# Folding a relu into VectorE's last sums in a Fourier mixing and expert layer kernel

## The chip, the cores and the metric

The kernel runs on one core of one Trainium2 chip. The metric is device time in microseconds (us) of one execution of the whole program. The kernel before takes 2613.54 us, the median of three runs between 2612.62 and 2613.75.

## What is computed

```python
def _attn_ref(x, w_r, w_i, b_r, b_i):          # x: 8 x 3008 x 256
    X = np.fft.rfft(x, axis=1)
    Yr = Xr @ w_r - Xi @ w_i + b_r
    Yi = Xr @ w_i + Xi @ w_r + b_i
    # soft threshold of both by 0.01
    y = np.fft.irfft(Y, n=x.shape[1], axis=1)

def _moe_ref(x, w_in, w_out):                  # 24064 tokens, 256 -> 2048 -> 256
    h = x @ w_in
    r = np.maximum(h, 0.0)
    g = r * r
    return g @ w_out
```

A Fourier transform over the sequence, a complex 256 by 256 mixing of each frequency, a soft threshold and the way back make the tokens. A two-layer network with a squared relu follows. Only that squared relu is touched by the change.

## The kernel before: tiles, stages and order

**The Fourier part** is done by small matrices on TensorE. A front stage, roughly the first 130 us, loads and converts the weights and handles batch 0. From then on, the Fourier work of batch b+1 (classes `Fwd`, `Pair`) and the last Fourier step of the tokens to come (`Back`, `Tokens`) run in between the network's work on batch b. In a `Pair`, `shrink` (lines 317 to 326) makes on VectorE the tile `kv` out of PSUM (line 322), clamps it to `kc` (line 324) and subtracts `kv - kc` in SBUF (through the helper at line 101). The next pair's `fwd` makes `kxl` on VectorE, from which TensorE's mixing products (line 301) take their low parts.

**The network** works on a token tile of 2h tokens (h is 250 or 252; 48 tiles) and, for each, on eight `Step`s of two blocks of 128 hidden units, 384 steps in all. fp32 values are split into a high and a low fp32r part, so each product takes three matmuls. The first layer's 2 by 2 block product is done with seven products instead of eight (21 matmuls of 250 or 252 columns per step, line 484 on TensorE, into the PSUM tiles `psh0` to `psh3`), and VectorE sums the seven products to the four quarters of the hidden tile `c` (tile `mc`, 128 partitions by 4h, three buffers):

- `first` (line 531): four products; then on VectorE a copy `p1` (`mp`), the sum `u2` (`mu`), the sum `v` (`mv`, 2h wide) and `c[:, 3]` (line 545, h wide).
- `second` (line 547): three products; then on VectorE `c[:, 1:3]` (line 553, 2h wide) and `c[:, 0]` (line 554, h wide). In the profile these three sums are `mc<-psh,mv` and `mc<-psh,mp`.
- Then ScalarE makes, over all 4h elements of `c`, relu in place (line 559), square in place (line 560) and a cast to fp32r, `g[0]` (tile `mg`, through `copy` at line 97). GpSimd (POOL in the profile) makes the low part `g[1] = c - g[0]` in two halves (`sub`, line 101).
- `out` (line 566): two times six matmuls of 500 or 504 columns into the accumulators `pso`.

**The order.** TensorE works on `first` of step n, then `out` of step n-2, then `second` of step n. The helper `then` (line 482) queues every instruction of the steps on its engine behind the last one of the steps; so the profile shows line 484 or the helper's lines 97, 98 and 101 for them. All other work (pairs, forward and back transforms) is traced in the order of a list of due times, and which of the instructions that are ready is put next into an engine's queue is decided when the program is built, by a scheduler that follows a model of the chip in time (`schedule_with_timeline_sim=True`, line 835). A queue is worked off in its order.

Of the kernel before, what the change touches and what calls it, by code (L numbers as in the profile page):

```python
# [8 lines left out]

F32 = mybir.dt.float32  # L10
F32R = mybir.dt.float32r
# [2 lines left out]
AF = mybir.ActivationFunctionType  # L14
# [44 lines left out]
def fnet_moe(ctx: ExitStack, tc, x, w_r, w_i, b_r, b_i, w_in, w_out, bm, cm, dx, a32, c32, out):  # L59
    nc = tc.nc  # L60
    pe, act, dve, pool = nc.tensor, nc.scalar, nc.vector, nc.gpsimd
# [3 lines left out]
    s1 = [dram.tile([G, NP1, 2, D], F32, name=f"s1_{b}") for b in range(B)]  # L65
# [22 lines left out]
    def T(name, shape, dt, tag=None):  # L88
        tag = tag or name
        return pools.get(tag, phase["pool"]).tile(shape, dt, name=name, tag=tag, bufs=phase["bufs"].get(tag, 2))  # L90

    def bank(shape, name="psf"):
        return phase["psum"].tile(shape, F32, name=name, tag=name, bufs=phase["bufs"].get(name, 1))

    def copy(eng, out, in_):
        if eng is act:
            return act.copy(out=out, in_=in_)  # L97
        return eng.tensor_copy(out=out, in_=in_)  # L98

    def sub(eng, out, a, b):  # L100
        return eng.tensor_tensor(out=out, in0=a, in1=b, op=ALU.subtract)  # L101
# [12 lines left out]
    def load_mix_weights():  # L114
        b32 = T("b32", [128, D], F32)
        for j, v in enumerate((b_r, b_i)):
            with tc.issue_after(ring[3].folds[1].ins):
                pool.dma_start(b32[64 * j:64 * j + 64, :], v.unsqueeze(0).broadcast_to([64, D]))
        for j, w in enumerate((w_r, w_i)):
            st = T(f"w32{j}", [128, 2, D], F32)  # L120
            w32.append(st)
            nc.sync.dma_start(st, w.rearrange("(c p) d -> p c d", p=128))
        wd = T("wd", [128, 2, D], F32, tag="small")
        wn = T("wn", [128, 2, D], F32, tag="small")
        sub(dve, wd, w32[1], w32[0])
        dve.scalar_tensor_tensor(out=wn, in0=w32[0], scalar=-1.0, in1=w32[1], op0=ALU.mult, op1=ALU.subtract)
        for j, w in enumerate((wd, wn, w32[0])):
            copy(act, wx[0][:, j], w)
            sub(dve, wx[1][:, j], w, wx[0][:, j])
        return b32  # L130
# [37 lines left out]
    def halves(hi, lo, v, eng):  # L168
        copy(act, hi, v)
        sub(eng, lo, v, hi)  # L170
# [33 lines left out]
    class Fwd:  # L204
# [28 lines left out]
        def run(self):  # L233
            ps = bank([128, 2, D])
            for t in range(2):
                nc.tensor.matmul(ps[:M1, t], am32[:, t], self.u[:, t], start=True, stop=True)  # L236
            self.ev = T("xe", [M1, 1, 2, D], F32)
            copy(act, self.ev[:, 0], ps[:M1])
            self.store()
# [242 lines left out]
    def then(eng, op, *args, **kwargs):  # L482
        with tc.issue_after(last_of[eng].ins) if eng in last_of else nullcontext():
            last_of[eng] = op(*args, **kwargs)  # L484
# [37 lines left out]
    class Step:  # L522
# [8 lines left out]
        def first(self):  # L531
            h = self.h
            self.ps = pa, pb, pc, pd = [bank([128, 2, 256], f"psh{j}")[:, :, :h] for j in range(4)]
            self.p1 = p1 = T("mp", [128, HM], F32)[:, :h]
            u2 = T("mu", [128, HM], F32)[:, :h]
            self.v = v = T("mv", [128, 2 * HM], F32)[:, :2 * h].rearrange("p (j h) -> p j h", j=2)
            self.c = c = T("mc", [128, 4 * HM], F32)[:, :4 * h].rearrange("p (j h) -> p j h", j=4)
            self.product(pa[:, 0], A11, B11)
            self.product(pa[:, 1], S2, T2)
            self.product(pb[:, 0], S1, T1)  # L540
            self.product(pb[:, 1], S3, T3)
            then(dve, copy, dve, p1, pa[:, 0])
            then(dve, dve.tensor_add, out=u2, in0=pa[:, 1], in1=p1)
            then(dve, dve.tensor_add, out=v, in0=pb, in1=u2.unsqueeze(1).broadcast_to([128, 2, h]))
            then(dve, dve.tensor_add, out=c[:, 3], in0=pb[:, 0], in1=v[:, 1])

        def second(self):
            h, c = self.h, self.c
            pc, pd = self.ps[2:]
            self.product(pc[:, 0], S4, B22)  # L550
            self.product(pc[:, 1], A22, T4)
            self.product(pd[:, 0], A12, B21)
            then(dve, dve.tensor_add, out=c[:, 1:3], in0=pc, in1=self.v)
            then(dve, dve.tensor_add, out=c[:, 0], in0=pd[:, 0], in1=self.p1)
            self.cut = last_of[dve]
            self.g = g = [
                T(f"mg{j}", [128, 4 * HM], F32R)[:, :4 * h].rearrange("p (j h) -> p j h", j=4) for j in range(2)
            ]
            then(act, act.activation, c, c, AF.Relu)
            then(act, act.activation, c, c, AF.Square)  # L560
            then(act, copy, act, g[0], c)
            self.done = last_of[act]
            for j in (slice(0, 2), slice(2, 4)):
                then(pool, sub, pool, g[1][:, j], c[:, j], g[0][:, j])
# [154 lines left out]
    for m in range(2 * len(steps) + 4):  # L719
        b, r = divmod(m, slots)  # L720
        if r == 0 and b < B:
            jobs = [(t - slots, job) for t, job in jobs]
            if b + 1 < B:
                first, step, end = 1.0, 6.1, 7.1
                if b == 0:
                    first, step, end = 11.2, 5.3, 9.1
                    for q in range(PRE, J):
                        if q > PRE + 1:
                            jobs += [(0.9 * (q - PRE - 2), second[q].load)]
                        jobs += [(0.5 + 0.9 * (q - PRE), second[q].run)]  # L730
                    jobs += [(first - 0.6, pairs[1][0].load)]
                jobs += pair_tasks(pairs[b + 1], first, step, end)
            if b + 2 < B:
                first, step = (2.6, 7.0) if b else (14.6, 6.0)
                jobs += fwd_tasks(b + 2, first, step) + [(95.0, pairs[b + 2][0].load)]
            for j in range(len(HALF)):
                t = b * len(HALF) + j + 1
                if t < len(tiles):
                    jobs += back_tasks(t, NF * j + 0.5)
            jobs.sort(key=lambda j: j[0])  # L740
# [16 lines left out]
def _float(bits):  # L757
    return float(np.array(bits, np.uint32).view(np.float32))
# [82 lines left out]
```

## Time and profile before

| | |
|---|---|
| median of three runs | 2613.54 us (2612.62 to 2613.75) |
| span of the profiled execution | 2611.6 us |
| what the runs have around such a span | 1.0 to 2.2 us |
| TensorE matmuls (PE) busy | 2565.9 us, 98% |
| VectorE (DVE) busy | 1788.3 us, 68% |
| ScalarE (ACT) busy | 1672.8 us, 64% |
| GpSimd (POOL) busy | 1658.6 us, 64% |
| mean granted TensorE clock | 0.995 |

An engine's row of the profile gives its busy time; the groups of instructions give count, busy time, mean duration and the idle time of the engine before them with what ended it. The waits list who waited for whom. The timeline shows instructions in order of time: start, duration, engine (PE is TensorE's matmuls, PEld its weight loads), line, operation, output and inputs, with the idle time before it in brackets. The profiled execution's own time, apart from its span, is not listed; the three runs lie 1.0 to 2.2 us over the span.

### The profile page before, as it was taken

The page shows a single profiled execution, that of the slowest core. Times are in us where ns is not written, and L with a number is a line of the kernel's source. Part 1 is how long each engine was busy: PE and PEld are TensorE (multiplying, and loading weights), DVE is VectorE, ACT ScalarE, POOL GpSimd, SP SyncE. Part 2 cuts the span into 40 slices and gives each one's busy share as a digit, 9 for nine tenths or more (in the row PEclk, how much of TensorE's full clock was granted, in tenths as well). Part 3 has the DMA queues.
Part 4 walks back from the last instruction along what each step waited for, and adds up shares of the span by engine and source line. Part 5 has one row for each costly group of instructions (what it writes and reads, how often), then busy time and mean ns, then how long its engine had stood idle before and what let it go on. Part 6 is the DMA issues. An engine that isn't in the chain of part 4 may idle for free.

```text
span 2611.6 us, 47553 instructions
## 1 busy us (share of the span) xinstructions
PE 2565.9 (98%) x16908; PEld 2347.7 (90%) x16908; DVE 1788.3 (68%) x3797; ACT 1672.8 (64%) x2434; POOL 1658.6 (64%) x1635
## 2 busy tenths in 40 slices
PE   6899999999999999999999999999999999999999
PEld 4789989999999999999999999999999999999998
DVE  7787766667767767577676776667676677765554
ACT  3566656666666666666666666666666666666665
POOL 2256666666766667667666676666667666666564
PEclk8999999999999999999999999999999999999999
DMA  8733332333332333233332333323332223221100
GB/s 265 253 100 106 102 113 80 96 108 104 94 94 78 113 104 88 82 95 114 103 92 82 97 110 100 100 76 100 104 106 82 69 81 101 72 65 40 34 17 17
DMA packets 191070, 250.51 MB, mean 96 GB/s; under 512 B 21790, under 2 KB 135958, under 8 KB 190834
## 3 DMA queue, kind: packets, MB, share of 16 engines
q1 hardware_dynamic: 177970, 223.40, 28.1%
q0 software_dynamic: 12864, 24.07, 3.9%
q8 instruction: 136, 2.23, 0.4%
q14 instruction: 100, 0.82, 0.1%
HBM read 146.85 MB, written 100.53 MB: 95 GB/s over the span
## 4 chain that ended last, share of the span: by engine, by line
PE 93%; DVE 3%; DMA 2%; POOL 1%; issue 1%; ACT 0%; SPq 0%; POOLq 0%; ACTq 0%; DVEq 0%
PE pso L484 39%; PE psh L484 35%; PE psf L301 7%; PE psf L280 3%; PE psf L236 2%; PE psf L333 2%; PE psf L464 1%; PE psf L465 1%; PE psf L461 1%; DMA du<-s 1%; DMA s<-xe 1%; PE psf L415 1%; PE psf L352 0%; DVE kv L101 0%; PE psf L373 0%
## 5 line engine op out<-in xcount | busy, mean ns | idle before, releaser
L101 POOL TENSOR_TENSOR mg<-mc,mg 128x500 fp32r<-128x500 f32 (+1 forms) x768 | 974.8, 1290 | 594.6 <-ACT mg L97 562.0
L484 PE MATMUL pso<-mg,wout 128*128 128x500 f32 (+1 forms) x4608 | 1176.2, 392 | 1.5 <-ACT mg L97 1.3
L484 PE MATMUL psh<-yt,win 128*128 128x250 f32 (+1 forms) x8064 | 1070.1, 281 | 1.6 <-DVE yr L471 1.0
L484 ACT ACTIVATE mc<-mc 128x1000 f32<-128x1000 f32 (+1 forms) x768 | 802.7, 1045 | 414.7 <-DVE mc L484 405.9
L484 PEld LDWEIGHTS psh<-yt,win 128*128 128x128 f32 x8064 | 1020.5, 189 | 33.9 <-PE psh L484 2.0
L484 PEld LDWEIGHTS pso<-mg,wout 128*128 128x128 f32 x4608 | 818.6, 189 | 130.0 <-POOL mg L101 2.0
L484 DVE TENSOR_TENSOR mc<-psh,mv 128x500 f32<-128x500 f32 (+3 forms) x768 | 419.6, 548 | 432.2 <-PE psh L484 399.7
L97 ACT CAST mg<-mc 128x1000 fp32r<-128x1000 f32 (+1 forms) x384 | 397.0, 1034 | 18.3
L484 DVE TENSOR_TENSOR mv<-psh,mu 128x500 f32<-128x500 f32 (+1 forms) x384 | 260.8, 679 | 55.3 <-PE psh L484 22.4
L301 PE MATMUL psf<-wx,kxh 128*128 128x256 f32 x1008 | 207.2, 282 | 1.6 <-ACT xe L97 0.7
L98 DVE COPY mp<-psh 128x250 f32<-128x250 f32 (+1 forms) x384 | 159.9, 416 | 32.5 <-PE psh L484 8.9
L101 POOL TENSOR_TENSOR ksl<-kv,ksh 128x512 fp32r<-128x512 f32 x84 | 108.7, 1294 | 100.6 <-ACT ksh L97 100.5
L301 PEld LDWEIGHTS psf<-wx,kxh 128*128 128x128 f32 x1008 | 166.6, 189 | 6.3 <-ACT xe L97 0.9
L484 DVE TENSOR_TENSOR mu<-psh,mp 128x250 f32<-128x250 f32 (+1 forms) x384 | 160.7, 418 | 11.5
L484 DVE TENSOR_TENSOR mc<-psh,mp 128x250 f32<-128x250 f32 (+1 forms) x384 | 157.1, 409 | 5.8 <-PE psh L484 4.2
L215 POOL TENSOR_TENSOR xs<-xt 120x256 f32<-120x256 f32 x156 | 114.9, 757 | 67.3 <-DMA xt<-x_in 66.6
L322 DVE TENSOR_TENSOR kv<-psf,ke 64x256 f32<-64x256 f32 x336 | 141.8, 422 | 18.1 <-PE psf L301 10.0
L301 PE MATMUL psf<-wx,kxl 128*128 128x256 f32 x504 | 141.5, 281 | 3.6 <-DVE kxl L101 3.6
L97 ACT COPY dy<-psf 128x188 f32<-128x188 f32 x256 | 77.0, 313 | 83.6 <-PE psf L465 82.7
L97 ACT CAST ksh<-kv 128x512 fp32r<-128x512 f32 x84 | 52.1, 620 | 118.0 <-DVE kv L101 117.2
L313 DVE TENSOR_TENSOR ke<-psf,bias 128x512 f32<-128x512 f32 x84 | 58.1, 691 | 100.6 <-PE psf L301 100.2
L97 ACT CAST kuh<-psf 128x256 fp32r<-128x256 f32 x192 | 68.3, 372 | 87.8 <-PE psf L333 72.5
(103 smaller groups left out, 2575.0 us busy)
## 6 DMA issues: line engine op xcount, KB each, us to landing
du<-s SPq DMA_DIRECT2D x128, 256.0 KB, 2.8
s<-kuh SPq DMA_DIRECT2D x192, 128.0 KB, 1.8
s<-kul SPq DMA_DIRECT2D x192, 128.0 KB, 2.0
ka<-s SPq DMA_DIRECT2D x84, 256.0 KB, 3.4
kcm<-cm_in POOLq DMA_DIRECT2D x84, 256.0 KB, 3.3
s<-xe SPq DMA_DIRECT2D x85, 240.0 KB, 2.4
xt<-x_in SPq DMA_DIRECT2D x84, 240.0 KB, 3.4
du<-s SPq DMA_DIRECT2D x256, 64.0 KB, 2.8
```

What stands on the lines that cost most here:

```text
L97: return act.copy(out=out, in_=in_)
L98: return eng.tensor_copy(out=out, in_=in_)
L101: return eng.tensor_tensor(out=out, in0=a, in1=b, op=ALU.subtract)
L215: return eng.tensor_tensor(out=out[:, :n], in0=self.xt[:, :n, 0], in1=self.xt[:, :n, 1], op=(ALU.add, ALU.subtract)[t])
L236: nc.tensor.matmul(ps[:M1, t], am32[:, t], self.u[:, t], start=True, stop=True)
L280: nc.tensor.matmul(pv[:, :, c, g, :], self.a[:, g, c * 128:(c + 1) * 128], bg, start=True, stop=True)
L301: self.last = nc.tensor.matmul(ps, l, wx[j][:, k, c, :], start=n == 0, stop=n == 5)
L313: dve.tensor_add(out=self.e, in0=self.pe, in1=bias)
L322: dve.tensor_add(out=v[64 * r:64 * r + 64, g], in0=ps[gs], in1=self.e[gs, r])
L333: nc.tensor.matmul(ps[:, :D], self.cm[:, g, j * 128:(j + 1) * 128], r[:, g], start=n == 0, stop=n == 2)
L415: nc.tensor.matmul(ps[:, :D], self.x[:, c, js], w32[j][:, c], start=n == 0, stop=n == 3)
L484: last_of[eng] = op(*args, **kwargs)
```

## The change

The three sums that write `c` become one VectorE instruction each that adds and clamps: it gives max(min(in0 + in1, 3.4e38), 0). ScalarE's relu over `c` is dropped; square and cast stay. The instruction is a program of its own for VectorE, not one of its stock operations. No tile, buffer, load or matmul is changed.

```diff
+from concourse.dve_ops import TENSOR_ADD_SAT
...
+    def add_relu(out, in0, in1):
+        return dve._custom_dve(TENSOR_ADD_SAT, out=out, in0=in0, in1=in1, s0=_float(0x7F7FFFFF), s1=0.0)
+
...
-            then(dve, dve.tensor_add, out=c[:, 3], in0=pb[:, 0], in1=v[:, 1])
+            then(dve, add_relu, out=c[:, 3], in0=pb[:, 0], in1=v[:, 1])
...
-            then(dve, dve.tensor_add, out=c[:, 1:3], in0=pc, in1=self.v)
-            then(dve, dve.tensor_add, out=c[:, 0], in0=pd[:, 0], in1=self.p1)
+            then(dve, add_relu, out=c[:, 1:3], in0=pc, in1=self.v)
+            then(dve, add_relu, out=c[:, 0], in0=pd[:, 0], in1=self.p1)
...
-            then(act, act.activation, c, c, AF.Relu)
             then(act, act.activation, c, c, AF.Square)
             then(act, copy, act, g[0], c)
```

## The prediction

> **What bounds the kernel now.** I read the profile's head first, then the chain of work that ended last, then what TensorE itself waited for, then stretches of time.
>
> ```profile
> span 2611.6 us, 47553 instructions
> PE 2565.9 (98%) x16908; PEld 2347.7 (90%) x16908; DVE 1788.3 (68%) x3797; ACT 1672.8 (64%) x2434; POOL 1658.6 (64%) x1635
> ...
> PE 93%; DVE 3%; DMA 2%; POOL 1%; issue 1%; ACT 0%; SPq 0%; POOLq 0%; ACTq 0%; DVEq 0%
> ```
>
> TensorE (PE) is busy for 98% of the span, and 93% of the chain is its matmuls; ScalarE (ACT), where the relu lies, has 0%. The span leaves TensorE 2611.6 - 2565.9 = 45.7 us of idle time. Next is where that time lies: busy time of each engine by stretch, in the order PE, PEld, DVE, ACT, POOL, then granted clock.
>
> ```profile
> 0.00:128.00 128.00, 98.31 (x435) 78.40 (x436) 95.75 (x197) 56.77 (x146) 36.28 (x43) 0.94 0.84 261
> 346.00:372.00 26.00, 20.18 (x125) 17.95 (x124) 15.67 (x29) 11.30 (x19) 17.76 (x20) 0.87 0.30 86
> 470.00:1000.00 530.00, 529.97 (x3580) 489.28 (x3579) 368.69 (x786) 345.00 (x503) 358.17 (x357) 1.00 0.34 100
> 2000.00:2400.00 400.00, 400.00 (x2700) 369.06 (x2699) 270.48 (x589) 264.57 (x372) 254.12 (x241) 1.00 0.24 72
> ```
>
> The front stage, where no `Step` runs yet, holds 128.00 - 98.31 = 29.7 us of it. A single stretch of 26 us in batch 0 holds another 5.8 us, at a clock of 0.87. In the long middle TensorE stands still for 0.03 us in 530 and not at all in 400. What it waited for from 128 us on (total, times, longest):
>
> ```profile
> PE psf L301 <- DVE kxl L101: 3.6, 3, 2.6
> PE psf L280 <- issue: 1.6, 1, 1.6
> PE psf L465 <- DMA du<-s: 1.5, 2, 1.0
> PE pso L484 <- ACT mg L97: 1.3, 1, 1.3
> PE psh L484 <- DVE yr L471: 1.0, 1, 1.0
> PE psf L301 <- ACT xe L97: 0.7, 1, 0.7
> ...
> PE pso L484 <- POOL mg L101: 0.2, 1, 0.2
> ```
>
> The only waits on the chain relu, square, cast, low part are one of 1.3 us and one of 0.2 us. So the output matmuls find their inputs ready in all 384 steps but one.
>
> **The change part by part. The relu.**
>
> ```profile
> L484 ACT ACTIVATE mc<-mc x768: 1031/1043/1098, 139.5 to 2601.8; 128x1000 f32<-128x1000 f32 x128, 128x1008 f32<-128x1008 f32 x64
> ```
>
> Relu and square are 768 instructions of 1.043 us (the middle figure). Half of them go: 384 x 1.043 = 400 us of ScalarE, a quarter of its 1672.8 us. That is a latency of 1.04 us per step which today lies beside TensorE's work, so in the middle of the kernel it is worth nothing. It is worth something where TensorE has run out of other work, at the end:
>
> ```profile
> 2599.71 0.68 DVE L484 TENSOR_TENSOR mc<-psh,mv 128x500 f32<-128x500 f32 x1 [1.86 <-PE psh L484]
> 2599.86 2.86 PE L484 MATMUL pso<-mg,wout 128*128 128x500 f32 x12
> 2600.31 0.41 DVE L484 TENSOR_TENSOR mc<-psh,mp 128x250 f32<-128x250 f32 x1
> 2600.75 2.11 ACT L484 ACTIVATE mc<-mc 128x1000 f32<-128x1000 f32 x2 [1.96 <-DVE mc L484]
> 2602.93 1.02 ACT L97 CAST mg<-mc 128x1000 fp32r<-128x1000 f32 x1
> 2604.01 1.17 PE L484 MATMUL pso<-mg,wout 128*128 128x500 f32 x4 [1.30 <-ACT mg L97]
> 2604.04 2.48 POOL L101 TENSOR_TENSOR mg<-mc,mg 128x500 fp32r<-128x500 f32 x2 [2.66 <-ACT mg L97]
> 2605.35 2.07 PE L484 MATMUL pso<-mg,wout 128*128 128x500 f32 x8 [0.17 <-POOL mg L101]
> ```
>
> The last step goes sums, relu, square, cast, low part, matmuls, one behind the other. Two ACTIVATEs take 2.11 us, so without one the cast ends 2.11 / 2 = 1.05 us earlier, at 2602.90. TensorE's twelve matmuls before it end at 2599.86 + 2.86 = 2602.72, so it can start then, and POOL's low part and the last eight matmuls move along. **The tail gives 1.05 us.** What is late next there is the same chain, now led by the square.
>
> **The sums.** Each step has one of 500 or 504 columns and two of half that. Their price as plain additions, and the nearest rows for an instruction that does more per element:
>
> ```profile
> L484 DVE TENSOR_TENSOR mc<-psh,mv 128x500 f32<-128x500 f32 x256 | 173.4, 677 | 279.1 <-PE psh L484 278.0
> L484 DVE TENSOR_TENSOR mc<-psh,mv 128x250 f32<-128x250 f32 x256 | 106.7, 417 | 21.6 <-ACT mc L484 0.5
> L484 DVE TENSOR_TENSOR mc<-psh,mp 128x250 f32<-128x250 f32 x256 | 104.6, 409 | 1.5
> L101 DVE TENSOR_TENSOR kv<-kv,kc 128x512 f32<-128x512 f32 x84 | 80.5, 958 | 0.7
> L159 DVE SCALAR_TENSOR_TENSOR dw<-dst,da 128x512 f32<-128x512 uint32 x16 | 10.8, 682 | 0.0
> L313 DVE TENSOR_TENSOR ke<-psf,bias 128x512 f32<-128x512 f32 x84 | 58.1, 691 | 100.6 <-PE psf L301 100.2
> ```
>
> They cost 677 + 417 + 409 = 1.503 us per step. No run shows the add-and-clamp program. The two-operation instruction of line 159 takes 682 ns where the one-operation sum of line 313 takes 691 for the same 512 columns: a second arithmetic step costs nothing, and I take nothing for a third. No VectorE row with a PSUM input is cheaper per column than the plain sum, so I exclude a gain. The upper bound from a row is the subtraction with both inputs in SBUF, 958 against 691, or +39%: +0.58 us per step. What would hide it is VectorE's own idle time: between steps with nothing else in them, it waits 1.86 us for products (the first sum of the tail above), and over 470 to 1000 us it is idle for 530 - 368.69 = 161 us, which at (2599.7 - 139.5) / 384 = 6.4 us per step is 1.9 us per step. Cover gone, every further microsecond per step would be 384 us.
>
> [...] The dear subtraction is dear in a particular way: it is drawn out in some executions only, and the sums never are (min/middle/max ns).
>
> ```profile
> L101 DVE TENSOR_TENSOR kv<-kv,kc x108: 410/683/2867, 41.5 to 2289.0; 128x512 f32<-128x512 f32 x84, 128x256 f32<-128x256 f32 x24
> L484 DVE TENSOR_TENSOR mc<-psh,mv x768: 403/542/685, 138.1 to 2599.7; 128x250 f32<-128x250 f32 x128, 128x252 f32<-128x252 f32 x64
> L101 POOL TENSOR_TENSOR mg<-mc,mg 128x500 fp32r<-128x500 f32 x512 | 647.2, 1285 | 376.5 <-ACT mg L97 356.7 <-DVE mv L484 11.2 <-DVE mu L484 7.6
> ```
>
> [...]
>
> **The order of the queues.** Nothing is moved by hand, but the instructions outside the steps are placed by the scheduler, whose model of time loses a relu per step. So their order past 138 us may differ, on TensorE, VectorE, ScalarE, POOL and the DMA queues alike. In the long middle no order shown costs TensorE anything. In batch 0 it does, once:
>
> ```profile
> 355.95 1.13 PE L280 MATMUL psf<-kb,ka 128*128 128x128 f32 x8 [1.55 <-issue]
> 357.58 2.44 POOL L101 TENSOR_TENSOR mg<-mc,mg 128x500 fp32r<-128x500 f32 x2
> 357.71 2.87 DVE L101 TENSOR_TENSOR kv<-kv,kc 128x512 f32<-128x512 f32 x1
> 360.50 0.68 DVE L101 TENSOR_TENSOR kxl<-psf,kxh 128x512 fp32r<-128x512 f32 x1
> 361.24 0.58 PE L301 MATMUL psf<-wx,kxl 128*128 128x256 f32 x1 [2.62 <-DVE kxl L101]
> ```
>
> POOL's two low-part subtractions hold off VectorE's `kv - kc` until 360.02; `kxl` is queued behind it, and TensorE waits 2.62 us for `kxl`. This subtraction is the longest of its kind, so a shift of POOL's pair by a microsecond most likely meets it worse placed for a collision. I count one POOL subtraction less ahead of it, 1.29 us. That is a guess at a size between 0 (the collision stays) and the whole stretch.
>
> **Sum.** Tail 1.05 + collision 1.29 = 2.3 us. Against the profiled span of 2611.6 us that is 2609.3; the three runs lie 1.0 to 2.2 us over that span, and I put it on their median: 2613.54 - 2.3 = **2611.2 us**. About 0.2%, 5.2 us, is what a measurement of this kernel can tell from no change, so the forecast is no change that can be told.
>
> **Rivals.**
>
> *The bad stretch goes.* A new order or timing dissolves all of 346 to 372 us: 5.8 us of idle time, and the clock of 0.87 over 26 us, whose 3.4 us of lost clock fall partly on the idle time; half of that makes 7.5 us in all. 2613.54 - 1.05 - 7.5 = 2605.0, faster. For it: the conjunction is the only one in 2250 us. Against it: two of its waits (1.55 and 0.7 us) have to do with pairs placed close behind one another in batch 0, which stays.
>
> *A second bad stretch.* The new order makes another in batch 0, where pairs stand closest: POOL's two subtractions start just ahead of a `kv - kc` in front of a `kxl`, TensorE waits over 2 us and its clock falls. Price 7.5 us again: 2613.54 - 1.05 + 7.5 = 2620.0, slower by 0.25%. It decides from a second stretch that costs 6.3 us, with the old one still there. Against it: half of the 108 subtractions take 683 ns or less, and the one in that stretch is the longest.
>
> *The sums become slow.* If the program runs at a fraction of the rate, or is shut out by POOL, VectorE becomes the bound beyond 1.86 us more per step, which is 2.2 times the present 1.503. At three times: (3.0 - 1.86) x 384 = 438 us, 3051 us. If each of the three waited out one POOL subtraction of 1.285 us: (3.86 - 1.86) x 384 = 768 us. For it: no row shows the program. Against it: line 159.
>
> *The waits are hidden.* TensorE's busy time is partly modelled, so ScalarE could hold it up unseen.
>
> ```profile
> L484 PEld LDWEIGHTS pso<-mg,wout 128*128 128x128 f32 x4608 | 818.6, 189 | 130.0 <-POOL mg L101 2.0
> ```
>
> The 130.0 us in which the weight loads of the output matmuls idle would then go: 2483 us. Against it: only 2.0 us are put down to anyone, and the pace of twelve bare matmuls, 2.86 / 12 = 0.238 us at most, is slower than a load of 0.189, so loads must idle. [...]
>
> **How the numbers follow.** Forecast 0.60 (2608.5 to 2616, the collision unchanged or gone, and the sums up to 0.58 us per step dearer with a few waits of that size); the bad stretch goes 0.25; a second one 0.10; slow sums 0.04; hidden waits 0.01. Faster: 0.25 + 0.01 = 0.26; same 0.60; slower 0.14. The range from 2603 to 2617 holds the first two cases, 0.85, and leaves a little for their edges.
>
> **What would show it.** In the profile of the changed kernel: 384 ACTIVATEs on `mc` and ScalarE near 1270 us; sums of 677, 417 and 409 ns with a maximum under 700; VectorE's busy time within a few microseconds of 1788; TensorE at 2566 us, with no waits past 470 us but in the tail; the first matmuls on the last `mg` 1.05 us closer to the last sum. Wrong would be: sums over 0.95 us for 500 columns, TensorE waiting for `mc` or `psh` tiles in the middle, or a change of TensorE's busy time by more than 10 us.

## The result

The kernel after takes 2633.99 us (median of 4 runs, 2629.59 to 2636.46), the kernel before 2613.64 us beside it (4 runs, 2612.62 to 2616.27): a ratio of 1.0078, with a 95% interval of 1.0064 to 1.0092. The change makes the kernel slower by 20.35 us, 0.8%; the forecast was 2611.2 us, no change that can be told, with a range up to 2617.

Lines have moved: the copy helper of line 97 is 98 after the change, and what lay behind the new helper is four lines further down (484 is 488, 101 is 105, 324 is 328, 333 is 337); the sums are now shown by the line of their helper, 102. First the head and the summary of the chain, of the profiled execution of the kernel after (2629.59 us).

```profile
span 2627.5 us, 47126 instructions
PE 2568.5 (98%) x16908; PEld 2348.4 (89%) x16908; DVE 1775.4 (68%) x3797; ACT 1305.1 (50%) x2050; POOL 1655.1 (63%) x1635
...
PE 88%; DVE 5%; DMA 2%; POOL 2%; issue 1%; ACT 0%; SPq 0%; POOLq 0%; DVEq 0%; ACTq 0%
```

The span is 2627.5 - 2611.6 = 15.9 us longer. TensorE's idle time has grown from 45.7 to 2627.5 - 2568.5 = 59.0 us, 13.3 us more, and its busy time by 2.6 us. In the chain, matmuls have gone from 93% to 88%, and VectorE and POOL have gained. (The median lies 4.4 us above this execution; what follows explains the 15.9 us of its span.) Next the stretches of time of the kernel after, columns as in the prediction.

```profile
128.00:470.00 342.00, 335.51 (x2211) 306.97 (x2212) 245.61 (x514) 171.87 (x272) 219.00 (x219) 0.99 0.35 101
470.00:1000.00 530.00, 527.35 (x3546) 486.36 (x3545) 360.23 (x777) 266.81 (x419) 352.76 (x354) 1.00 0.33 98
1000.00:1500.00 500.00, 495.66 (x3316) 455.73 (x3315) 336.54 (x720) 251.44 (x387) 328.69 (x327) 1.00 0.32 94
1500.00:2000.00 500.00, 494.39 (x3328) 455.70 (x3328) 343.84 (x736) 252.03 (x394) 333.32 (x337) 1.00 0.33 95
2000.00:2400.00 400.00, 395.89 (x2651) 364.89 (x2650) 264.73 (x580) 198.39 (x302) 249.97 (x239) 0.99 0.25 75
```

And three of them before:

```profile
128.00:470.00 342.00, 332.03 (x2177) 303.47 (x2177) 247.12 (x514) 215.88 (x319) 213.80 (x215) 0.98 0.35 100
1000.00:1500.00 500.00, 499.83 (x3353) 460.26 (x3352) 342.38 (x727) 327.85 (x470) 334.42 (x332) 1.00 0.32 94
1500.00:2000.00 500.00, 499.79 (x3362) 460.91 (x3362) 347.43 (x739) 327.10 (x474) 338.46 (x339) 1.00 0.34 98
```

Batch 0 has become better: from 128 to 470 us TensorE idles 6.5 us in place of 10.0. But the long middle, without idle time before, now idles 2.65 + 4.34 + 5.61 + 4.11 = 16.7 us between 470 and 2400 us, against 0.4. The waits of TensorE from 128 us on (total, times, longest) say for what:

```profile
PE psf L337 <- ACT ksh L98: 11.3, 6, 4.0
PE psh L488 <- DVE mc L102: 3.2, 6, 1.3
PE psf L305 <- POOL kxl L105: 2.8, 5, 1.0
...
PE pso L488 <- ACT mg L98: 0.2, 1, 0.2
PE pso L488 <- POOL mg L105: 0.2, 1, 0.2
```

There are six waits on `ksh` (the high part of a pair's result, which the back products of that pair at line 337 take), and they come once in each of six batches, in its tenth pair: the back products start late at 684.1, 1003.1, 1320.7, 1639.5 and 1957.8 us, by 1.45 to 1.47 us each, and at 2265.4 us, in the last batch, by 3.96 us. Behind each of the first five comes a wait of 0.36 or 0.37 us for `mc`, and 8 us ahead of each one of 0.39 to 0.96 us for `kxl`. The relu's own chain, up to `mg`, delays nothing in the middle. Neither do the sums by themselves (the five waits for `mc` go when the stall in front of them is taken away, in the last run below). Here are their groups (count, busy time, mean ns, idle time before):

```profile
L102 DVE CUSTOM_DVE_ANT_0 mc<-psh,mv 128x500 f32<-128x500 f32 x256 | 173.2, 677 | 245.6 <-PE psh L488 245.0
L102 DVE CUSTOM_DVE_ANT_0 mc<-psh,mv 128x250 f32<-128x250 f32 x256 | 106.6, 416 | 27.2 <-DVE mv L488 4.6 <-POOL xs L219 0.2 <-POOL yt L105 0.2
L102 DVE CUSTOM_DVE_ANT_0 mc<-psh,mp 128x250 f32<-128x250 f32 x256 | 104.7, 409 | 0.3
```

677, 416 and 409 ns: add-and-clamp costs what the plain sum cost. And the 400 us are gone from ScalarE (min/middle/max ns):

```profile
L102 DVE CUSTOM_DVE_ANT_0 mc<-psh,mv x768: 400/542/685, 136.2 to 2616.8; 128x250 f32<-128x250 f32 x128, 128x252 f32<-128x252 f32 x64
...
L488 ACT ACTIVATE mc<-mc x384: 1035/1042/1067, 137.6 to 2617.8; 128x1000 f32<-128x1000 f32 x128, 128x1008 f32<-128x1008 f32 x64
```

So every part that the edit names did what was forecast, and the loss came from elsewhere. This is the timeline of the kernel after at the tenth pair of one batch, weight loads and other rows left out:

```profile
997.76 2.88 PE L488 MATMUL pso<-mg,wout 128*128 128x500 f32 x12
997.91 2.48 POOL L105 TENSOR_TENSOR mg<-mc,mg 128x500 fp32r<-128x500 f32 x2
998.43 2.95 DVE L328 TENSOR_SCALAR kc<-kv 128x512 f32<-128x512 f32 x1
...
1000.36 0.73 POOL L219 TENSOR_TENSOR xs<-xt 120x256 f32<-120x256 f32 x1
...
1000.48 1.20 PE L488 MATMUL psh<-yt,win 128*128 128x250 f32 x9
1001.41 0.42 DVE L99 COPY mp<-psh 128x250 f32<-128x250 f32 x1
1001.75 0.68 DVE L105 TENSOR_TENSOR kv<-kv,kc 128x512 f32<-128x512 f32 x1
...
1002.46 0.62 ACT L98 CAST ksh<-kv 128x512 fp32r<-128x512 f32 x1 [4.45 <-DVE kv L105]
...
1003.13 0.85 PE L337 MATMUL psf<-ksh,kcm 128*128 128x256 f32 x4 [1.45 <-ACT ksh L98]
```

VectorE's clamp `kc` starts while POOL makes its low-part pair, and takes 2.95 us; it ends only after POOL's `xs`, which follows the pair at once. `kv - kc`, queued behind it and behind the copy `mp`, is late, `ksh` is late, and the back products, which the queue of TensorE has right behind the nine matmuls of `second`, wait 1.45 us. The tenth pair of the following batch before the change (in the kernel after it looks like the one above, with a clamp of 3.30 us):

```profile
1310.56 2.66 POOL L101 TENSOR_TENSOR mg<-mc,mg 128x500 fp32r<-128x500 f32 x2 [0.17 <-ACT mg L97]
...
1310.92 1.18 DVE L324 TENSOR_SCALAR kc<-kv 128x512 f32<-128x512 f32 x1
...
1312.13 2.60 PE L484 MATMUL psh<-yt,win 128*128 128x250 f32 x21
1312.35 1.42 DVE L101 TENSOR_TENSOR kv<-kv,kc 128x512 f32<-128x512 f32 x1
...
1313.80 0.62 ACT L97 CAST ksh<-kv 128x512 fp32r<-128x512 f32 x1 [1.96 <-DVE kv L101]
...
1314.57 0.84 PE L484 MATMUL pso<-mg,wout 128*128 128x500 f32 x3
...
1315.25 0.40 PE L333 MATMUL psf<-ksh,kcm 128*128 128x256 f32 x2
```

Here clamp and subtraction run into POOL's pair too (1.18 and 1.42 us), but the clamp starts earlier against TensorE's work: `ksh` ends at 1314.42 and is asked for at 1315.25, with 0.83 us to spare, since TensorE has 21 matmuls of `first` and `second` and three of `out` in front. That is how the two queue orders differ. Two theories followed from this reading. **Order:** the scheduler, with one instruction less per step in its model, lays out other queues, and those hold a stall that comes back in each batch. **Timing:** with the shorter chain, POOL's pair itself comes at another time, in any order. Third, the **program:** the new VectorE instruction disturbs something that its own rows do not show.

### The profile page after: what moved, and what is told of

Its sections match the earlier page's. It is cut to its first block, busy times and chain, and to the rows that moved or that the text cites. A ratio compares the mean times of both kernels' runs of the same rounds, so it can differ in the third digit from the quotient of the medians.

```text
span 2627.5 us, 47126 instructions
## 1 busy us (share of the span) xinstructions
PE 2568.5 (98%) x16908; PEld 2348.4 (89%) x16908; DVE 1775.4 (68%) x3797; ACT 1305.1 (50%) x2050; POOL 1655.1 (63%) x1635
## 4 chain that ended last, share of the span: by engine, by line
PE 88%; DVE 5%; DMA 2%; POOL 2%; issue 1%; ACT 0%; SPq 0%; POOLq 0%; DVEq 0%; ACTq 0%
PE pso L488 38%; PE psh L488 34%; PE psf L305 6%; PE psf L284 2%; PE psf L240 2%; PE psf L337 2%; PE psf L468 1%; PE psf L469 1%; DMA xt<-x_in 1%; PE psf L465 1%; POOL mg L105 1%; DVE kc L328 1%; DVE kv L105 0%; DMA s<-xe 0%; DMA x<-x_in 0%
## 5 line engine op out<-in xcount | busy, mean ns | idle before, releaser
L105 POOL TENSOR_TENSOR mg<-mc,mg 128x500 fp32r<-128x500 f32 (+1 forms) x768 | 965.0, 1277 | 602.6 <-ACT mg L98 542.2
L488 PE MATMUL pso<-mg,wout 128*128 128x500 f32 (+1 forms) x4608 | 1159.4, 392 | 0.4 <-ACT mg L98 0.2
L102 DVE CUSTOM_DVE_ANT_0 mc<-psh,mv 128x500 f32<-128x500 f32 (+3 forms) x768 | 419.2, 548 | 412.6 <-PE psh L488 370.0
L488 ACT ACTIVATE mc<-mc 128x1000 f32<-128x1000 f32 (+1 forms) x384 | 400.8, 1044 | 478.3 <-DVE mc L102 477.3
L102 DVE CUSTOM_DVE_ANT_0 mc<-psh,mp 128x250 f32<-128x250 f32 (+1 forms) x384 | 157.2, 409 | 1.8 <-PE psh L488 1.4
L475 DVE TENSOR_TENSOR yr<-psf,dy 128x188 f32<-128x188 f32 (+4 forms) x256 | 78.3, 313 | 74.5 <-ACT dy L98 68.4
```

What stands on the lines that cost most here:

```text
L102: return dve._custom_dve(TENSOR_ADD_SAT, out=out, in0=in0, in1=in1, s0=_float(0x7F7FFFFF), s1=0.0)
L475: self.cut = dve.tensor_add(out=o, in0=ps[:, 0, lo:hi], in1=y[:, c, lo:hi])
```

## The experiments

Each ratio is against the kernel before, with a 95% interval.

**Both relus.** The program stays, and ScalarE's relu is put back; in the trace, all engines then work through their instructions in the order of the kernel before.

```diff
+            then(act, act.activation, c, c, AF.Relu)
             then(act, act.activation, c, c, AF.Square)
```

> The changed kernel with ScalarE's relu kept as well (it clamps what is clamped already, so the output is the same). Every queue then has exactly the order of the kernel before; only the three sums are the add-and-clamp program. Theory 'order' (the loss comes from the new order of the queues): 2613.5 us, within 2 us of before. Theory 'timing' (the loss comes from ScalarE's chain being 1.04 us shorter on the chip): 2613.5 us too. Theory 'program' (the add-and-clamp program itself costs something that its own rows don't show): about 2630 us.

Measured: 2612.52 us (2610.41 to 2615.87, 10 runs) beside 2612.56, ratio 1.000 (0.9991 to 1.001). In the order of before, the program by itself costs nothing.

**Plain sums, no relu.** The other half alone: plain additions, and the relu left out of the computation. The queues have exactly the order of the kernel after.

```diff
-            then(dve, add_relu, out=c[:, 3], in0=pb[:, 0], in1=v[:, 1])
+            then(dve, dve.tensor_add, out=c[:, 3], in0=pb[:, 0], in1=v[:, 1])
...
-            then(dve, add_relu, out=c[:, 1:3], in0=pc, in1=self.v)
-            then(dve, add_relu, out=c[:, 0], in0=pd[:, 0], in1=self.p1)
+            then(dve, dve.tensor_add, out=c[:, 1:3], in0=pc, in1=self.v)
+            then(dve, dve.tensor_add, out=c[:, 0], in0=pd[:, 0], in1=self.p1)
```

> The changed kernel with plain additions in place of the add-and-clamp program; the relu is left out altogether, so the output is that of h squared. Every queue has exactly the order of the changed kernel. 'Order' and 'timing': 2630 to 2636 us, as the changed kernel. 'Program': 2612.5 us.

Measured: 2632.06 us (2631.09 to 2639.65), ratio 1.0084 (1.0068 to 1.01). The whole loss, without the program. What remains is the missing ScalarE instruction, by order or by timing.

**The order of before with a short relu.** The relu is planned in full size, so that the queues come out as before the change, and cut to 2 of its 1000 or 1008 columns when they are laid out; the sums clamp.

```diff
+            then(act, act.activation, c, c, AF.Relu)
...
+    _resized_relu(nc, 2)     # after the queues are laid out: relu on 2 columns
```

> The changed kernel, with a relu on ScalarE traced and scheduled at full size, so that every queue has the order of before, and then cut to two columns per step when the program is finished (it clamps what is clamped already). On the chip ScalarE's chain is some 0.85 us shorter per step than before. 'Order': 2612.7 us, that is 2613.5 less 0.85 us in the tail. 'Timing': the collision of the tenth pair of each batch comes back and the time is 2622 us or more.

Measured: 2609.56 us (2606.66 to 2613.05, 10 runs), ratio 0.9991 (0.9981 to 1.0). With the order held, the change is worth 3.0 us; the prediction's sum was 2.3. The shorter chain does act on the collision: the clamp of the tenth pair now takes 1.78 to 2.19 us in the five batches that have the waits of 1.45 us in the kernel after (0.83 to 1.19 before the change). But `ksh` is still ready 0.55 to 0.67 us before TensorE asks for it, so nothing is lost.

**The order of after with a long chain.** The reverse: the order of the kernel after, with an instruction of the relu's size put ahead of every square on ScalarE (it reads `c` and writes a spare tile).

```diff
+    _extra_act(nc)     # after the queues are laid out: relu of c into a spare tile ahead of each square
```

> The changed kernel with an extra ScalarE instruction of the relu's size in front of each square, put in when the program is finished, so that every queue keeps the order of the changed kernel (the extra one reads c and writes a spare tile that nobody reads). On the chip ScalarE's chain is as long as before. 'Order': 2631 to 2637 us, the changed kernel's time plus 1.05 us of tail. 'Timing': the collision goes and the time is 2613 to 2620 us.

Measured: 2641.1 us (2636.35 to 2641.67), ratio 1.0106 (1.009 to 1.0123), with six waits for `ksh` at the same places (five of 1.07 to 1.45 us and one of 4.28). That is 4 us over the range of 'order', too; where those come from was not traced. The loss stays with the order and does not go with the relu's time: the theory of timing, as the cause of the loss, falls from both sides.

**The clamp in PSUM.** Before the change the sums, with an input in PSUM, took 685 ns at most, and `kv - kc`, all in SBUF, up to 2867. To take the clamp out of POOL's way, `kc` is written into the PSUM bank of its product. This changes what is traced, and so the order is drawn anew.

```diff
-            ps = bank([128, 512])[:, :D]
+            bk = bank([128, 512])
+            ps = bk[:, :D]
...
-            cl = T("kc", [128, 2, D], F32, tag="ke")
+            cl = bk.rearrange("p (g d) -> p g d", g=2)
```

> The changed kernel with the clamp kc of shrink written into the PSUM bank of its product in place of an SBUF tile, so that neither the clamp nor kv - kc has two sides in SBUF. The order of the queues is drawn anew. Theory 'collision' (what the new order costs is VectorE's clamp held off by POOL in the tenth pair, so that TensorE waits for ksh behind it): clamp and subtraction take the same time each time (under 0.75 us), the waits on ksh go, and the time falls to 2605 to 2616 us. Theory 'place' (what costs is only where the back products stand in TensorE's queue): no reason to fall; 2625 to 2640 us, or anything that a new order gives.

Measured: 2639.49 us (2635.63 to 2640.42), ratio 1.0095 (1.008 to 1.0111). The durations came as 'collision' said (min/middle/max ns):

```profile
L329 DVE TENSOR_SCALAR psf<-kv x84: 681/684/696, 187.7 to 2317.1; 128x512 f32<-128x512 f32 x84
L105 DVE TENSOR_TENSOR kv<-kv,psf x84: 672/677/689, 188.6 to 2318.7; 128x512 f32<-128x512 f32 x84
```

With one side in PSUM, neither instruction takes over 696 ns in any of the 84 pairs. The time is a miss: the waits for `ksh` are gone, but others come back in their place, for `yt`, `ke`, `kp` and `kul`. What the collision costs in the order of the kernel after can't be read from this run, since it has two changes in it, the clamp's place and the order.

**Back products due later.** In the list of due times, a pair's back products get 8.5 in place of 7.1, and in a second run 7.7.

```diff
-                first, step, end = 1.0, 6.1, 7.1
+                first, step, end = 1.0, 6.1, 8.5
```

> The changed kernel with the due time of a pair's two back products 1.4 half-steps later from batch 1 on (8.5 in place of 7.1), nothing else. The order is drawn anew; in it the back products of the pairs stand up to a step later. 'Place': the waits on ksh go, 2605 to 2616 us. 'Collision': the clamp is still held off where it falls behind POOL's pair, but less hangs on it; 2608 to 2625 us.

Measured: 2655.9 us (2653.29 to 2657.84), ratio 1.016 (1.0145 to 1.0176); no wait for `ksh`, but this line at the head of TensorE's waits, and more behind it:

```profile
PE psf L305 <- DVE kxl L105: 12.6, 6, 2.5
```

Both theories missed it: room for the back products was given, and another step of the pair was late, once in each of five batches by 2.46 to 2.48 us.

> The changed kernel with that due time 7.7 in place of 7.1. In the tenth pair the back products then stand six matmuls of 0.117 us later, 0.7 us, against a wait of 1.46 us. 'Place': the wait halves to 0.7 us and per batch some 1 us is won: 2622 to 2630 us. 'Collision': as here, unless the new order moves the clamp away from POOL's pair; then below 2616 us.

Measured with 7.7: 2613.08 us (2609.61 to 2615.89, 10 runs), ratio 0.9999 (0.9989 to 1.0008). Nothing over 0.2 us comes back from batch to batch; the clamp of the tenth pair takes 0.51 us in the batch that is shown above for the kernel after. The whole change with another draw of the order costs nothing.

> The kernel before with the same due time of 7.7: its work is unchanged and only the order is drawn anew. If the order of before is one draw among many, this moves the time by several us to either side, 2605 to 2630 us; if only the missing relu makes a bad order, it stays within 3 us of 2612.5 us.

Measured, the kernel before with 7.7: 2612.32 us (2610.35 to 2616.66, 10 runs), ratio 0.9999 (0.9989 to 1.0008). So 7.7 is no better setting by itself. The queues do differ from those of before, and the time stayed within 3 us: by its own forecast this run speaks for 'only the missing relu makes a bad order'. The next one tests that again.

**The kernel before with 8.5.**

> The kernel before with the pairs' back products due 8.5 instead of 7.1, the setting with which the kernel after took 2655.9 us. Theory 'a draw' (any queue order can hold a stall that comes back in every batch, with the relu or without): no figure follows for this one; anything from 2611 to 2660 us, and if it is over 2620, the trace shows a stall at the same place of several batches. Rival 'the missing relu' (only without the relu in the planner's model does such a stall arise): 2608 to 2618 us with no stall that comes back, and the 8.5 is harmless by itself.

Measured: 2626.79 us (2624.51 to 2629.18), ratio 1.0056 (1.004 to 1.0072). The relu is there, and still a stall comes back, in every second batch: TensorE waits 0.84 us for `mc` at 565.1, 1198.6 and 1832.5 us. So a bad order does not need the missing relu. TensorE's idle time between 470 and 2400 us is 2.06 + 1.56 + 2.12 + 1.83 = 7.6 us, against 0.4 before; the time is 13.6 us longer, so the waits are not all of it.

**The kernel after with 7.4.**

> The kernel after with the pairs' back products due 7.4, halfway between 7.1 (2634 us) and 7.7 (2613 us). Theory 'a draw' (the order is drawn anew by any change of the settings, and the time goes by whether a stall comes back in each batch): either near 2613 us without a stall that comes back, or over 2622 us with one, which need not be in the tenth pair; not in between with the same three waits halved. Rival 'too early' (7.1 asks for the back products too early and each tenth of a due time later gives some slack): 2618 to 2628 us, with the tenth pair's wait on ksh at half its 1.45 us.

Measured: 2612.81 us (2610.59 to 2615.47, 10 runs), ratio 1.0003 (0.9994 to 1.0012), and no wait for `ksh`. It is not halfway, so 'too early' falls. But it is no further draw either: in the traces, all engines work through the same instructions in the same order as with 7.7, so this is that run once more. Whether orders without the relu are worse on the whole stays open: of three orders with it one cost 14 us, and of four without it three cost 20 to 43 us (one of these has the clamp in PSUM as well).

**The order of after, with a clamp that POOL does not hold off.** What the PSUM run was meant to test, now with the order held: when the queues are laid out, the clamp's input becomes 3 rows of 170 columns and its output one row of 510 (it and the subtraction behind it leave out 2 of 512 columns). That POOL does not hold off a clamp of this shape was not shown by any run before this one.

```diff
+    n = 2 * D - 2
...
+                src = copy_replace(src, ap=[src.ap[0], (170, 3), (1, 170)], bass_ap=None)
+                dst = copy_replace(dst, ap=[dst.ap[0], (1, n)], bass_ap=None)
```

> [...] Theory 'collision' (in the tenth pair of each batch VectorE's clamp is held off by GpSimd's two low-part subtractions and the xs behind them): the clamp takes 0.55 to 0.75 us in every pair, also in the tenth, where it took 2.95 us; TensorE's wait there for ksh falls from 1.45 us to 0.5 us or less and the one for mc (0.36) goes; 2615 to 2626 us. Rival 'place' (kv - kc is too late in VectorE's queue whatever the clamp takes, because it stands behind the step's first copy or is itself held off): the clamp is short, but the waits stay over 1 us each; 2630 to 2637 us.

Measured: 2625.81 us (2625.0 to 2627.32), ratio 1.005 (1.0037 to 1.0062). That is 12.6 us over the kernel before beside it (2613.2), where the kernel after lies 20.4 over its own: 7.7 us are gone (the intervals of the two, 0.37 to 0.62% and 0.64 to 0.92%, do not meet). The rows of `kc`, `kv` and the tenth pair:

```profile
L106 DVE TENSOR_TENSOR kv<-kv,kc x108: 410/682/2525, 41.2 to 2303.2; 128x510 f32<-128x510 f32 x84, 128x256 f32<-128x256 f32 x24
L329 DVE TENSOR_SCALAR kc<-kv x84: 673/677/686, 190.1 to 2301.8; 128x510 f32<-128x510 f32 x84
```

```profile
998.54 0.69 DVE L329 TENSOR_SCALAR kc<-kv 128x510 f32<-128x510 f32 x1
...
999.60 2.18 DVE L106 TENSOR_TENSOR kv<-kv,kc 128x510 f32<-128x510 f32 x1
...
1002.48 0.85 PE L338 MATMUL psf<-ksh,kcm 128*128 128x256 f32 x4 [0.69 <-ACT ksh L99]
```

The clamp now takes 673 to 686 ns everywhere (min/middle/max). But the subtraction, which came after POOL's work in the kernel after, now runs into it and takes 2.18 us; so the back products still wait 0.67 to 0.69 us in the five batches, and the wait of 0.36 us for `mc` stays. 'Collision' has the time and the clamp right, but not the two waits; 'place' named the subtraction's being held off as one way to lose, but not the time. The collision is real, and it moved on to the next instruction.

**Neither is held off.** As the run before, and a second clamp of the same kind, from `kc` to `kv`, stands in the place of the subtraction, which is left out.

```diff
+                src = copy_replace(i.ins[1], ap=[i.ins[1].ap[0], (170, 3), (1, 170)], bass_ap=None)
+                dst = copy_replace(i.outs[0], ap=[i.outs[0].ap[0], (1, n)], bass_ap=None)
...
+                i = copy_replace(clamp, ins=(src, *clamp.ins[1:]), outs=(dst,), **{k: getattr(i, k) for k in keep})
```

> As the run with the clamp in one row (the kernel after in its own queue order), and in the place of the subtraction kv - kc, in which GpSimd's low-part pair now held VectorE up for 2.18 us in the tenth pair, a second clamp of the same one-row kind from kc to kv, with a single input in SBUF: the soft threshold's subtraction is left out (and 2 of 512 columns, as there), so that neither instruction can be held off by GpSimd. Theory 'collision' (the whole of the stall that comes back is these two instructions held off by GpSimd): both instructions take 0.68 us in all 84 pairs; in the tenth pair kv is ready about 1.5 us earlier than with the clamp alone, ksh is there before TensorE asks for it, no wait on ksh or mc comes back in the batches, and the time is 2613 to 2618 us, within 0.2% of the kernel before. Rival 'place' (the rest of the loss, 12.6 us of 20.4, comes from where the new order puts the work, not from these two): the waits on ksh and mc in the tenth pair stay at over half of what the clamp alone left, and the time is 2621 to 2627 us.

Measured: 2616.37 us (2613.9 to 2618.77, 11 runs) beside 2613.21, ratio 1.0013 (1.0004 to 1.0022): 3.2 us over the kernel before. The rows of both instructions, then the first of TensorE's waits:

```profile
L329 DVE TENSOR_SCALAR kc<-kv x84: 673/677/686, 187.7 to 2292.4; 128x510 f32<-128x510 f32 x84
L106 DVE TENSOR_SCALAR kv<-kc x84: 673/676/686, 188.6 to 2293.7; 128x510 f32<-128x510 f32 x84
```

```profile
PE psf L338 <- ACT ksh L99: 3.5, 1, 3.5
```

The five waits of 1.45 us are gone in the same queue order, and with them the five for `mc`: the theory of the collision holds for them. Of the five waits for `kxl` (2.8 us) two are left (1.1 us). Together that is 7.3 + 1.8 + 1.7 = 10.8 us, of the 2627.5 - 2614.6 = 12.9 us by which the two profiled executions differ. One wait for `ksh` is left, in the last batch (3.96 us in the kernel after), and it is no collision:

```profile
2248.30 0.47 PE L489 MATMUL psh<-yt,win 128*128 128x250 f32 x2
...
2249.23 0.68 DVE L329 TENSOR_SCALAR kc<-kv 128x510 f32<-128x510 f32 x1
...
2249.95 0.69 DVE L106 TENSOR_TENSOR kxl<-psf,kxh 128x512 fp32r<-128x512 f32 x1
...
2250.89 0.68 DVE L106 TENSOR_SCALAR kv<-kc 128x510 f32<-128x510 f32 x1
...
2252.26 1.22 PE L338 MATMUL psf<-ksh,kcm 128*128 128x256 f32 x4 [3.49 <-ACT ksh L99]
```

TensorE's queue has only two matmuls of the steps ahead of the back products there, and VectorE's queue has `kxl` and `kp` ahead of the last step of `kv`. That is a bad place in the order. Its 3.49 us are of the size of the 3.2 us that this run keeps over the kernel before; that the one makes the other is argued, not shown.

## Why the prediction was wrong

**The parts that were right.** The price of the sums (677, 416 and 409 ns against 677, 417 and 409; none of the 1152 took over 685 ns, before or after). The 400 us of ScalarE, hidden: the group of ACTIVATEs falls from 768 to 384 instructions of the same length. ScalarE's busy time falls by 1672.8 - 1305.1 = 367.7 us only, where I had put some 400, because the records of neighbouring instructions overlap in part and the busy time counts an overlap once (ScalarE's groups add up to 1778.6 us before and 1377.2 after, 105.8 and 72.1 us more than its busy time); the ACTIVATEs on `mc` by themselves fall from 802.7 to 400.8 us. The tail, in the kernel after:

```profile
2617.35 0.41 DVE L102 CUSTOM_DVE_ANT_0 mc<-psh,mp 128x250 f32<-128x250 f32 x1
2617.79 1.04 ACT L488 ACTIVATE mc<-mc 128x1000 f32<-128x1000 f32 x1 [3.03 <-DVE mc L102]
...
2619.99 1.17 PE L488 MATMUL pso<-mg,wout 128*128 128x500 f32 x4 [0.23 <-ACT mg L98]
```

From the last sum to the first matmul on its `mg` it is 2619.99 - 2617.35 = 2.64 us, where it was 3.70: 1.06 us closer, forecast 1.05. And the sum, 2.3 us, agrees with the run with the order of before (3.0 us), though with an interval from 0 to 5 us that is no sharp test. In its profile TensorE's wait for `kxl` in batch 0, put at 1.29 us less as a guess, falls from 2.62 to 0.40 us, but a wait of 1.86 us for `yt` comes up just ahead of it; in all, TensorE idles 1.9 us less between 128 and 470 us. The term had the right sign, by another path than the one named, and that its size was near is luck.

**The step that failed** is "the order of the queues". It saw that the order could differ on every engine, and then said: "In the long middle no order shown costs TensorE anything. In batch 0 it does, once." The second half of that is a reading of one order, and the first half made it a property of the kernel. So the sum put the middle at nothing for every order, where the order of the kernel after costs TensorE 16.7 - 0.4 = 16.3 us more idle time between 470 and 2400 us. The middle repeats itself batch by batch, and the order that is bad at the tenth pair is bad there in six batches, in five of them by the collision. The rival of "a second bad stretch" had the mechanism, POOL's two subtractions just ahead of VectorE's work on a pair, and the sign; but it was placed in batch 0 only, priced once (7.5 us) and given 0.10. The victim was also another: it is the clamp, one step ahead of the subtraction that I watched, and TensorE's wait is for `ksh`, not for `kxl`. Its row before the change would have warned:

```profile
L324 DVE TENSOR_SCALAR kc<-kv x84: 417/556/3810, 190.1 to 2287.9; 128x512 f32<-128x512 f32 x84
```

A clamp of 417 ns that takes up to 3810: collisions were there before, in the middle too (the clamp that starts at 722.2 us takes 2.59), and TensorE's queue had enough work in front of the back products to hide each of them. What the forecast took for freedom from collisions was slack, in the tenth pair some tenths of a microsecond, as the 0.83 us above. The collisions have not even grown in sum: clamp and subtraction take 73.3 + 80.5 us of VectorE before and 75.0 + 67.3 us after (hence most of its 12.9 us less busy time). What changed is where one falls and how much slack stands behind it. One of the prediction's own signs of being wrong, TensorE waiting for `mc` in the middle, did show, as five waits of 0.36 us behind the stalls.

**What is shown and what is argued.** Shown: the program is free; the loss goes with the queue order and not with the relu's time; another draw of the order with the same change loses nothing (one order, met with 7.7 and with 7.4); in the order of the kernel after, taking the two VectorE instructions out of POOL's way, in all pairs, wins back 20.4 - 3.2 = 17.2 us, 7.7 of it with the clamp alone; waits that can be named in the profiles make up 10.8 of it. Argued: that the scheduler's model does not hold VectorE off while POOL works, and so takes the tenth pair for one that is in time. Open: why the median of the kernel after lies 4.4 us over its profiled execution (two of the three longer runs have the same granted clock of 0.994). And no version was found that beats the kernel before by more than the measurement can tell; the nearest is the one with the order of before (0.9991).

## What to carry to other kernels

Where a planner lays out the queues, removing an instruction is two changes: the instruction's time, and a new order; hold the order in one run and the time in another before either is judged. A stall that costs nothing in one order has a slack that can be read (when an input is ready, when it is asked for), and a slack under the length of one collision means that the next order may lose it, once in every repetition. Price such a loss by the number of repetitions, not by the one place where it is seen.

## What the runs showed of the hardware

**A clamp that waits for three POOL instructions.** The clamp (one input, input and output in SBUF) takes 0.42 to 0.43 us in the 37 of 84 pairs of the kernel after in which no POOL instruction overlaps it. In the tenth pair it was held for POOL's pair and for the `xs` that followed at once: 2.95 us, and 3.30 us in the other four batches with the stall. Taken as 3 rows in and 1 row out, over 510 of the 512 columns, it takes 0.67 to 0.69 us in all 84 pairs, also in the tenth, where it starts 0.51 us into POOL's pair (998.54 against 998.03 us). What it is in this shape that keeps it from being held, no run shows.

**A lower clock beside short waits.** Stretches of the kernel after, around two of its waits (granted clock in the third column from the right):

```profile
684.00:692.00 8.00, 7.58 (x37) 6.66 (x38) 4.62 (x11) 3.47 (x6) 4.46 (x4) 0.79 0.00 1
2262.00:2272.00 10.00, 6.60 (x27) 5.90 (x28) 4.60 (x8) 1.13 (x3) 4.26 (x5) 0.66 0.19 54
```

In the 8 us that begin as the wait of 1.46 us ends and hold the one of 0.36 us, the granted clock was 0.79; around the wait of 3.96 us it was 0.66 over 10 us. The other four waits of 1.45 us drew no such stretch in this execution (1.00 in the 8 us from 1003, 1320, 1639 and 1957 us on), and before the change, with almost no waits in the middle, the clock was 1.00 there.
